# Gated Fourier mixing and attention on one core: fewer GpSimd transfers and a last head pair in two blocks

## The chip, the cores and the metric

The kernel runs on one core of a Trainium2 chip. The metric is the device time of one execution in microseconds (us), lower is better. TensorE (PE) multiplies, VectorE (DVE), ScalarE (ACT) and GpSimd (POOL) do the rest, SyncE (SP) and now and then ACT and POOL issue transfers. Each engine works off its own instructions in the order in which the program has them.

## The reference

One input x of 2048 rows and 512 columns goes through two branches that are mixed by a gate of each row:

```python
a = x @ dft_hid_re.T ; b = x @ dft_hid_im.T
y = dft_seq_re @ a - dft_seq_im @ b            # Fourier branch
q, k, v = split(x @ wqkv)                      # 32 heads of 16 columns
p = softmax(q @ k.T * 16**-0.5)                # 2048 x 2048 for each head
o = concat(p @ v) @ wo                         # attention branch
g = sigmoid((x * gate_w).sum(-1))
out = g * y + (1 - g) * o
```

All is float32. The kernel splits operands of most products into a high and a low part (`hi_lo`, L74), so one product of the reference is three on PE.

## The kernel before, in words

**Head pairs and units.** Two heads are a pair `p` (16 pairs). The stacks `qs[p % 2]` and `ks[p % 2]` hold the two heads in rows 0 to 49 and 64 to 113: 48 rows of high and low parts and two rows (48 and 49) that subtract the row's maximum. In `ks` these two rows are ones, written once (L282) before the first pair. In `qs` they are filled for each pair and each half of 1024 queries by `m_rows` (L262): DVE transposes the maxima into `mt`, then eight transfers of 2 KB (four blocks `b`, two heads `h`) go into the stack, those of head 0 from SP and those of head 1 from POOL.

A unit `u` is one pair, one half of the queries and one tile of 128 keys: 512 units (`UNITS`) in all. `scores` (L690) makes four score tiles of 128 keys by 512 queries for a unit, two heads by two query blocks, and ACT takes their exponential into `pt`. `pv` (L701) multiplies the four with the values, each into its own 32 columns of PE (four run side by side), and adds up in the PSUM bank `acc` over the 16 key tiles of a half. Row 16 of a head's values is one, so `acc` also has the sums for the softmax. Then ACT copies `acc` to `oe` and it goes to DRAM.

**PSUM.** Eight banks: three `s` (scores of head 0, and of both heads in the main part), three `a` (first maxima, at the end scores of head 1), one `acc`, one `d` (the products that fill the gaps).

**What fills the gaps.** Until unit 491 the maxima of the next pair and the Fourier branch run between the scores; `segment` places them by patterns. The results of the Fourier branch, already times the gate, are in `yg_d`. In the last part the attention's output is multiplied with `wo`, in column tiles `ct` of four pairs each: `proj(hf, cts, pools)` (L592) yields, for each of the eight row tiles of a half, three products for each `ct`, and `finish` (L583) takes the bank, scales it with 1 - g and adds it to the row tile `yp`. `first` is the half 0 with `ct` 0 to 2, `third` the half 1 with `ct` 3 without the last pair, `last` the half 0 with `ct` 3 (then the row tile is written out). `more` gives them the banks d, a, a in turn.

**The order at the end.** After the patterns four single scores remain, then the loop over u = 492, 494, ..., 510. I call one turn of it a section: half of the scores of two units, a number of products by the table `whole`, the other half, and the values of the two units before. `run_plan(u)` (L772) issues what is due: at 486 to 494 `last_block` for half 1, at 498 and 500 the sums and their reciprocals of the last column tile of half 0, at 506 its parts, at 500 `load_w15`, the four rows of `wo` that belong to the last pair.

**The last pair's second half** is not written to DRAM. `last_pair` copies `acc`, turns it so that queries are in the partitions, divides by the sums, turns it back, splits it in high and low, and multiplies with `w15`: eight row tiles, three products each, two at a time in two banks on two groups of 32 rows. Four of the eight tiles are scaled by ACT and added by POOL, the others by DVE, and SP writes all eight. Nine of `last`'s products are put between the steps, three more before the last step.

At the start `warm_up` (L131) lets DVE clear a tile, with which PE then multiplies nine times before the first inputs are there; POOL makes `ident`, the unit matrix.

Of the kernel before, what the change touches and what calls it, by code (L numbers as in the profile page):

```python
# [9 lines left out]
F32 = mybir.dt.float32  # L10
# [5 lines left out]
P = 128  # L16
# [15 lines left out]
def mix_kernel(ctx: ExitStack, tc: tile.TileContext, xa_t, xa, wqkv, w_hid, w_seq, wo, gate_w, out):  # L32
# [229 lines left out]
    def m_rows(p, hf):  # L262

        nc.vector.transpose(mt[hf], nhl[hf].rearrange("p v m -> p (v m)").bitcast(F32))  # L264
        for b in range(4):
            for h in range(2):
                rows = qs[p % 2][64 * h + 48:64 * h + 50, hf * 1024:(hf + 1) * 1024].bitcast(F32)
                (nc.sync, nc.gpsimd)[h].dma_start(rows.rearrange("v (q b c) -> v b q c", q=8, b=4)[:, b],  # L268
                                                  mt[hf][32 * b + h:32 * b + 32:2])

    def run_deferred():
        while deferred:
# [3 lines left out]
    ones = st1.tile([2, 2 * D], F32, name="hl", bufs=4)  # L276
    nc.gpsimd.memset(ones, 1.0)
    nc.gpsimd.memset(vt[:, :, :, 16:17], 1.0)
    for i in range(2):
        for h in range(2):  # L280
            for tb in range(2):
                nc.gpsimd.dma_start(ks[i][64 * h + 48:64 * h + 50, tb * 2 * D:(tb + 1) * 2 * D].bitcast(F32), ones)  # L282
    load_stacks(0)
    wos = [staged(wo[:, kt]) for kt in range(KT)]
    wrs = []
    a_next = 0

# [290 lines left out]
                parts(t[:, 0], t[:, 1], o)  # L578
                oh[hf, 3] = tiles(t)

    last_few = []

    def finish(ps, t, y, other=False):  # L583
        if other:

            tmp = last_few[0][:, t % 4]
            nc.scalar.activation(tmp, ps, AF.Copy, scale=omg[:, t:t + 1])
            nc.gpsimd.tensor_tensor(y, y, tmp, ALU.add)
            return
        nc.vector.scalar_tensor_tensor(y, ps, omg[:, t:t + 1], y, op0=ALU.mult, op1=ALU.add)  # L590

    def proj(hf, cts, pools):  # L592

        for qt in range(8):
            t = hf * 8 + qt
            chain = Chain(*pools[qt % len(pools)], 3 * len(cts))
            for ct in cts:
                h1, l1 = oh[hf, ct][qt]
                for i, (st, mv) in enumerate(((h1, 0), (h1, 1), (l1, 0))):
                    last = ct == cts[-1] and i == 2  # L600
                    yield chain, st, wos[0][:, mv, ct], partial(proj_next, hf, cts, t, chain) if last else None

    def proj_next(hf, cts, t, chain):
        finish(chain.ps, t, yp[t], last_few)
        if hf == 0 and cts[-1] == 3:
            nc.sync.dma_start(out[t * P:(t + 1) * P, :], yp[t])

# [14 lines left out]
    w15 = []  # L622

    def load_w15():
        w = work.tile([64, 2, D], F32R, name="w15")
        for i in range(4):
            nc.sync.dma_start(w[16 * i:16 * i + 16].bitcast(F32), wo_d[3][64 * (i % 2) + 3:64 * (i % 2) + 64:4])
        w15.append(w)

    def last_pair(fill):  # L630
        oe = work.tile([P, 4, P], F32, name="oe", bufs=2)
        on = work.tile([P, 4, 2, 2, DH], F32, name="on15")
        rc = work.tile([P, 4, 2, 2], F32, name="rc15")
        o15 = work.tile([64, 2, 4, P], F32R, name="o15", tag="pt", bufs=4)
        last_few.append(work.tile([P, 4, D], F32, name="few", tag="pt", bufs=4))
        w = w15[0]
        for c in range(4):
            nc.scalar.copy(oe[:, c], acc[:, c * P:(c + 1) * P])

        def turn(cs):  # L640
            t = psS.tile([P, 512], F32, name="s")
            for i, c in enumerate(cs):
                nc.tensor.transpose(t[:, i * P:(i + 1) * P], oe[:, c], ident)
            v = t[:, :2 * P].rearrange("p (c b r) -> p c b r", c=2, b=2)
            r = rc[:, cs.start:cs.stop]
            nc.vector.reciprocal(r, v[:, :, :, 16:48:16])
            for h in range(2):
                nc.vector.tensor_tensor(on[:, cs.start:cs.stop, :, h], v[:, :, :, 33 * h:33 * h + DH],
                                        r[:, :, :, h:h + 1].broadcast_to([P, 2, 2, DH]), ALU.mult)

        def back(cs):
            t = psS.tile([P, 512], F32, name="s")
            for i, c in enumerate(cs):
                nc.tensor.transpose(t[:64, i * P:(i + 1) * P], on[:, c].rearrange("p b h d -> p (b h d)"), ident)
            v = t[:64, :2 * P].rearrange("p (c q) -> p c q", c=2)
            hi_lo(o15[:, 0, cs.start:cs.stop], o15[:, 1, cs.start:cs.stop], v)

        lo, hi = range(0, 2), range(2, 4)
        pump(fill, 3)
        pump(fill, 3)  # L660
        turn(lo)
        turn(hi)
        back(lo)
        pump(fill, 3)
        back(hi)
        drain(fill)
        for c in range(4):
            pss = [(psA if b or c % 2 else psD).tile([P, 512], F32, name="a" if b or c % 2 else "d") for b in range(2)]
            for i, (st, mv) in enumerate(((0, 0), (0, 1), (1, 0))):
                for b in range(2):  # L670
                    rr = slice(32 * b, 32 * b + 32)
                    nc.tensor.matmul(pss[b], o15[rr, st, c], w[rr, mv], start=i == 0, stop=i == 2)
            for b in range(2):
                t = 8 + 4 * b + c
                y = yp.pop(t)
                finish(pss[b], t, y, b and c % 2 == 0)
                nc.sync.dma_start(out[t * P:(t + 1) * P, :], y)


    def gate():  # L680
# [9 lines left out]
    def scores(u, qb, h, other=False):  # L690
        p, r = divmod(u, 32)
        hf, kt = divmod(r, 16)
        q0 = hf * 1024 + qb * 512
        if u not in pts:
            pts[u] = work.tile([P, 4, 512], F32, name="pt", bufs=4)
        ps = psA.tile([P, 512], F32, name="a") if other else psS.tile([P, 512], F32, name="s")
        rr = slice(64 * h, 64 * h + 50)
        nc.tensor.matmul(ps, ks[p % 2][rr, kt * P:(kt + 1) * P], qs[p % 2][rr, q0:q0 + 512], start=True, stop=True)  # L698
        return nc.scalar.activation(pts[u][:, 2 * qb + h], ps, AF.Exp, bias=0.0, scale=DH ** -0.5)  # L699

    def pv(u, evac=True):  # L701
        p, r = divmod(u, 32)
        hf, kt = divmod(r, 16)
        pt = pts.pop(u)
        for j in range(4):
            h = j % 2
            nc.tensor.matmul(acc[32 * j:32 * j + 17], vt[:, kt, p, 16 * h:16 * h + 17], pt[:, j],  # L707
                             start=kt == 0, stop=kt == NT - 1)
        if kt == NT - 1 and evac:
# [216 lines left out]
```

## Time and profile before

| | us |
|---|---|
| three runs, median (lowest to highest) | 1725.36 (1724.99 to 1726.66) |
| the profiled execution | 1726.38 |
| its span, first to last instruction | 1724.3 |

| engine | busy us in the profiled execution | instructions |
|---|---|---|
| PE | 1713.2 | 13018 |
| DVE | 1364.3 | 2296 |
| ACT | 1149.4 | 2256 |
| POOL | 446.5 | 562 |

Times in the views are counted from the start of the span. A row of a timeline has the start, the length, the engine, the line, the operation and its tiles (out<-in), a count, and in brackets how long the engine stood idle before it and what ended that. "SPq" and "POOLq" rows, and POOL's DMA_DIRECT2D rows, are issues of transfers. The chain of waits is the path that ended last: start, length, engine, tile, line. PE's rows in a timeline overlap, as matmuls are pipelined; in the chain each has only what it adds.

### The profile page before, as it was taken

The numbers are of one execution on the slowest core, as the hardware profiler recorded it, in microseconds if no ns is written. First come the engines' busy times: TensorE is split into PE (matmuls) and PEld (weight loads), VectorE is DVE, ScalarE is ACT, GpSimd is POOL, SyncE is SP. The second block draws the span as 40 slices with busy tenths as digits, with TensorE's granted clock in tenths as the row PEclk, the third lists the DMA queues.
The fourth block names the chain that finished last, engine by engine and source line by source line (L and its number), as shares of the span: only waits on it lengthen the run. The fifth ranks groups of instructions, "written<-read, shape, count | busy, mean of one in ns | idle before, by whom it ended". The sixth has DMA issues, their size and how long they took to land.

```text
span 1724.3 us, 33482 instructions
## 1 busy us (share of the span) xinstructions
PE 1713.2 (99%) x13018; PEld 1043.1 (60%) x13018; DVE 1364.3 (79%) x2296; ACT 1149.4 (67%) x2256; POOL 446.5 (26%) x562
## 2 busy tenths in 40 slices
PE   9999999999999999999999999999999999999998
PEld 7888655456666666666666666666666666544443
DVE  5439788888888888888888888888888888799953
ACT  5211377777766777677767777777677777777776
POOL 0111121322222333222322333333232343200111
PEclk9999999999999999999999999999999999999999
DMA  8963500314141524214146535233141534460103
GB/s 290 347 145 141 136 7 14 44 38 75 56 75 45 96 87 101 72 35 78 39 92 246 114 100 104 62 66 66 45 89 61 125 100 93 169 153 24 39 27 129
DMA packets 82350, 164.82 MB, mean 96 GB/s; under 512 B 19712, under 2 KB 19968, under 8 KB 78352
## 3 DMA queue, kind: packets, MB, share of 16 engines
q1 hardware_dynamic: 77552, 161.77, 36.6%
q8 instruction: 102, 1.67, 0.4%
q0 software_dynamic: 4352, 0.39, 0.3%
q10 hardware_dynamic: 288, 0.52, 0.1%
q14 instruction: 56, 0.46, 0.1%
HBM read 107.47 MB, written 54.52 MB: 94 GB/s over the span
## 4 chain that ended last, share of the span: by engine, by line
PE 98%; DVE 0%; DMA 0%; ACT 0%; issue 0%; POOL 0%; DVEq 0%; ACTq 0%; POOLq 0%
PE d L410 35%; PE acc L707 28%; PE a L245 12%; PE s L698 12%; PE s L324 3%; PE s L356 1%; PE d L324 1%; PE a L81 1%; PE a L79 1%; PE s L81 1%; PE s L79 1%; PE a L80 1%; PE s L80 1%; PE a L410 0%; PE s L203 0%; PE a L203 0%
## 5 line engine op out<-in xcount | busy, mean ns | idle before, releaser
L247 DVE TENSOR_REDUCE mx<-a 128x1 f32<-128x512 f32 x2026 | 1246.4, 683 | 244.4 <-PE a L245 222.2
L699 ACT ACTIVATE pt<-s 128x512 f32<-128x512 f32 x2008 | 1024.1, 620 | 389.5 <-PE s L698 332.4
L245 PE MATMUL a<-ks,qs 48*128 48x512 f32 x2026 | 813.3, 416 | 0.0
L698 PE MATMUL s<-qs,ks 50*128 50x512 f32 x2008 | 770.0, 413 | 1.6 <-DMA qs<-mt 1.2
L410 PE MATMUL d<-xab,ch 64*128 64x512 f32 x2016 | 648.5, 396 | 0.0
L707 PE MATMUL acc<-pt,vt 128*17 128x512 f32 x4096 | 500.7, 596 | 0.0
L410 PEld LDWEIGHTS d<-xab,ch 64*128 64x128 f32 x2016 | 365.9, 184 | 126.9 <-DVE mx L247 60.4
L698 PEld LDWEIGHTS s<-qs,ks 50*128 50x128 f32 x2008 | 366.1, 184 | 111.0 <-ACT pt L699 33.7
L245 PEld LDWEIGHTS a<-ks,qs 48*128 48x128 f32 x2026 | 367.7, 185 | 66.8 <-DVE mx L247 40.2
L410 PE MATMUL d<-xab,cl 64*128 64x512 f32 x1008 | 399.3, 396 | 0.0
L410 PEld LDWEIGHTS d<-xab,cl 64*128 64x128 f32 x1008 | 185.4, 184 | 65.5 <-DVE mx L247 40.8
L394 POOL CAST ch<-craw 128x512 fp32r<-128x512 f32 x126 | 77.2, 612 | 558.3 <-PE s L698 192.0
L707 PEld LDWEIGHTS acc<-pt,vt 128*17 128x17 f32 x4096 | 90.6, 96 | 205.9 <-issue 205.9
L395 POOL TENSOR_TENSOR cl<-craw,ch 128x512 fp32r<-128x512 f32 x126 | 162.4, 1289 | 10.2
L268 POOL DMA_DIRECT2D qs<-mt x128 | 72.0, 568 | 158.2 <-DVE mt L264 150.0
L410 PE MATMUL d<-wre,xab 64*128 64x512 f32 (+1 forms) x348 | 93.9, 402 | 0.1
L410 PEld LDWEIGHTS d<-wre,xab 64*128 64x128 f32 (+1 forms) x348 | 60.0, 185 | 32.0 <-issue 23.6
L410 PE MATMUL d<-wo_hl,o_hl 64*128 64x512 f32 (+1 forms) x261 | 70.9, 397 | 0.0
L410 PEld LDWEIGHTS d<-wo_hl,o_hl 64*128 64x128 f32 (+1 forms) x261 | 47.2, 185 | 16.9 <-issue 11.7
L75 ACT CAST hl<-s 128x512 fp32r<-128x512 f32 x28 | 16.2, 588 | 59.7 <-PE d L324 25.2
L259 POOL CAST nhl<-nm 128x16 fp32r<-128x16 f32 x32 | 6.3, 197 | 160.8 <-DVE nm L256 160.8
L427 POOL CAST xab<-y 128x512 fp32r<-128x512 f32 x16 | 9.8, 610 | 129.8 <-ACT y L426 107.2
(147 smaller groups left out, 967.8 us busy)
## 6 DMA issues: line engine op xcount, KB each, us to landing
craw<-w_seq SPq DMA_DIRECT2D x128, 256.0 KB
qk<-hl SPq DMA_DIRECT2D x32, 512.0 KB
qs<-qk SPq DMA_DIRECT2D x96, 128.0 KB
ks<-qk SPq DMA_DIRECT2D x96, 128.0 KB
b<-hl SPq DMA_DIRECT2D x16, 512.0 KB
xab<-b SPq DMA_DIRECT2D x16, 512.0 KB
o<-oe SPq DMA_DIRECT2D x62, 128.0 KB
oh<-nh SPq DMA_DIRECT2D x12, 512.0 KB
```

The source lines that it names most:

```text
L79: nc.tensor.matmul(ps, sh, mh, start=first, stop=False)
L80: nc.tensor.matmul(ps, sh, ml, start=False, stop=False)
L245: nc.tensor.matmul(ps, qs[p % 2][r, qt * P:(qt + 1) * P], ks[p % 2][r, kb * 512:(kb + 1) * 512], start=True, stop=True)
L247: user = nc.vector.tensor_reduce(mx[p % 2][:, h, qt, kb:kb + 1], ps, AX.X, ALU.max)
L268: (nc.sync, nc.gpsimd)[h].dma_start(rows.rearrange("v (q b c) -> v b q c", q=8, b=4)[:, b], mt[hf][32 * b + h:32 * b + 32:2])
L324: i = nc.tensor.matmul(ps, st[r], mv[r], start=not half and not j, stop=half == 1 and j == 11)
L394: nc.gpsimd.tensor_copy(h1, raw)
L395: nc.gpsimd.tensor_tensor(l1, raw, h1.bitcast(F32), ALU.subtract)
L410: i = nc.tensor.matmul(self.ps, st[r], mv[r], start=not self.begun, stop=stop)
L698: nc.tensor.matmul(ps, ks[p % 2][rr, kt * P:(kt + 1) * P], qs[p % 2][rr, q0:q0 + 512], start=True, stop=True)
L699: return nc.scalar.activation(pts[u][:, 2 * qb + h], ps, AF.Exp, bias=0.0, scale=DH ** -0.5)
L707: nc.tensor.matmul(acc[32 * j:32 * j + 17], vt[:, kt, p, 16 * h:16 * h + 17], pt[:, j], start=kt == 0, stop=kt == NT - 1)
```

## The change

**Transfers.** The eight transfers of ones go from POOL to SP, behind the first pair's stacks. In `m_rows` POOL issues those of head 1 only if the group is neither the first nor the last of all, and for the first pair only three of four. So POOL issues 30 groups of four less one, 119 transfers in all, and SP issues the 17 others.

**The last sections.** `proj` gets a list of row tiles. `first` and `last` leave out row tile 7, which is done apart: three products (`early`) at 504 and nine (`late`) behind the last values. Five of `first`'s products go between the third and the fourth of the single scores. The table `whole` has other numbers.

**The last pair by blocks of 512 queries.** Units 496 to 511 run through all 16 key tiles for the first 512 queries and then for the second: a unit there is two key tiles by one query block, and `acc` holds, for each head, the even and the odd key tiles apart. A constant `pairsum`, two unit matrices of 64 one above the other, made by DVE, adds the two while the block is turned (`turn`). Block 0 (`LastPair(0)`) is copied after unit 503, turned in section 506, turned back in 508 and multiplied before the last two units' values; block 1 follows behind them. Its products use four groups of 32 rows, one for each row tile and each with its own bank, and `w15` stands four times in 128 partitions (eight transfers instead of four). One tile of block 1 goes by ACT and POOL and is written by ACT's queue, and the kept row tile 7 is added by DVE in between.

```diff
+    pairsum = const.tile([P, 64], F32, name="pairsum")
+    nc.vector.tensor_tensor(pairsum, ident[:, :64], ident[:, 64:], ALU.add)
...
+                own = h and 0 < 2 * p + hf < 2 * NP - 1 and (p or b < 3)
                 rows = qs[p % 2][64 * h + 48:64 * h + 50, hf * 1024:(hf + 1) * 1024].bitcast(F32)
-                (nc.sync, nc.gpsimd)[h].dma_start(rows.rearrange("v (q b c) -> v b q c", q=8, b=4)[:, b],
-                                                  mt[hf][32 * b + h:32 * b + 32:2])
+                (nc.gpsimd if own else nc.sync).dma_start(rows.rearrange("v (q b c) -> v b q c", q=8, b=4)[:, b],
+                                                            mt[hf][32 * b + h:32 * b + 32:2])
...
+    load_stacks(0)
+    wos = [staged(wo[:, kt]) for kt in range(KT)]
     for i in range(2):
         for h in range(2):
             for tb in range(2):
-                nc.gpsimd.dma_start(ks[i][64 * h + 48:64 * h + 50, tb * 2 * D:(tb + 1) * 2 * D].bitcast(F32), ones)
-    load_stacks(0)
-    wos = [staged(wo[:, kt]) for kt in range(KT)]
+                nc.sync.dma_start(ks[i][64 * h + 48:64 * h + 50, tb * 2 * D:(tb + 1) * 2 * D].bitcast(F32), ones)
...
+    class LastPair:
...
+        def copy(self, n):
+            for c in range(n):
+                cols = slice(c * 512 // n, (c + 1) * 512 // n)
+                nc.scalar.copy(self.oe[:, cols], acc[:, cols])
+
+        def turn(self):
+            t = self.bank(0)
+            for c in range(4):
+                nc.tensor.matmul(t[:, 64 * c:64 * c + 64], self.oe[:, c * P:(c + 1) * P], pairsum, start=True, stop=True)
+            v = t[:, :256].rearrange("p (c r) -> p c r", c=4)
+            nc.vector.reciprocal(self.rc, v[:, :, 16:48:16])
+            for h in range(2):
+                nc.vector.tensor_tensor(self.on[:, :, h], v[:, :, 33 * h:33 * h + DH],
+                                        self.rc[:, :, h:h + 1].broadcast_to([P, 4, DH]), ALU.mult)
+
+        def back(self):
+            t = self.bank(1)
+            nc.tensor.transpose(t[:, :P], self.on.rearrange("p c h d -> p (c h d)"), ident)
+            hi_lo(self.o15[:, 0], self.o15[:, 1], t[:, :P])
+
+        def products(self, pools, order, others=()):
+            pss = [pool.tile([P, 512], F32, name=name) for pool, name in pools]
+            for i, (st, mv) in enumerate(((0, 0), (0, 1), (1, 0))):
+                for c in range(4):
+                    r = slice(32 * c, 32 * c + 32)
+                    nc.tensor.matmul(pss[c], self.o15[r, st], w15[0][r, mv], start=i == 0, stop=i == 2)
+            for c in order:
+                t = 8 + 4 * self.blk + c
+                y = yp.pop(t)
+                finish(pss[c], t, y, c in others)
+                (nc.scalar if c in others else nc.sync).dma_start(out[t * P:(t + 1) * P, :], y)
...
     def last_pair(fill):
...
+        few.append(work.tile([P, D], F32, name="few", tag="pt", bufs=4))
+        x = LastPair(1, [(psS, "s")])
+        x.copy(4)
+        pump(fill, 1)
+        x.turn()
+        pump(fill, 5)
+        x.back()
         drain(fill)
+        x.products([(psA, "a")] * 3 + [(psD, "d")], (1, 2, 0, 3), (0,))
...
+        if u >= UNITS - 16:
+            blk, kt = divmod(kt, 8)
+            q0, kt = 1024 + blk * 512, 2 * kt + qb
...
+    def pv_last(u):
+        blk, k2 = divmod(u - UNITS + 16, 8)
+        pt = pts.pop(u)
+        for j in range(4):
+            x, h = divmod(j, 2)
+            nc.tensor.matmul(acc[32 * j:32 * j + 17], vt[:, 2 * k2 + x, NP - 1, 16 * h:16 * h + 17], pt[:, j],
+                             start=k2 == 0, stop=k2 == 7)
+        if blk == 0 and k2 == 7:
+            last_pairs.append(LastPair(0, [(psD, "d"), (psA, "a")]))
+            last_pairs[0].copy(1)
...
-    first = proj(0, (0, 1, 2), one)
+    first = proj(0, (0, 1, 2), one, range(7))
...
     for i in range(4):
+        if i == 3:
+            pump(first, 5)
         score("s", 1)
...
-    last = proj(0, (3,), more)
-    whole = {492: (first, 9), 494: (first, 9), 496: (first, 9), 498: (third, 6), 500: (third, 6), 502: (third, 6),
-             504: (third, 3), 506: (third, 3), 508: (last, 6), 510: (last, 6)}
+    last = proj(0, (3,), more, range(7))
+
+    early, late = proj(0, (0,), one, (7,)), proj(0, (1, 2, 3), [(psS, "s")], (7,))
+    whole = {492: (first, 4), 494: (first, 9), 496: (third, 9), 498: (third, 3), 500: (third, 9), 502: (third, 3),
+             504: (early, 3), 508: (last, 9), 510: (last, 12)}
...
-                pump(*whole[u])
+                pump(*whole.get(u, ((), 0)))
+                if u == 506:
+                    last_pairs[0].turn()
+                elif u == 508:
+                    last_pairs[0].back()
...
+    last_pairs[0].products([(psA, "a")] * 3 + [(psD, "d")], range(4))
     pv(UNITS - 2)
-    pv(UNITS - 1, evac=False)
-    last_pair(last)
+    pv(UNITS - 1)
+    last_pair(late)
```

More of the change, by code (lines that the diff above doesn't have):

```diff
@@ L579, in last_block @@
                 oh[hf, 3] = tiles(t)
-    last_few = []
+    few = []
     def finish(ps, t, y, other=False):
         if other:
-            tmp = last_few[0][:, t % 4]
+            tmp = few[0]
             nc.scalar.activation(tmp, ps, AF.Copy, scale=omg[:, t:t + 1])
@@ L590, in finish, with proj @@
         nc.vector.scalar_tensor_tensor(y, ps, omg[:, t:t + 1], y, op0=ALU.mult, op1=ALU.add)
-    def proj(hf, cts, pools):
-        for qt in range(8):
+    def proj(hf, cts, pools, qts=range(8)):
+        for qt in qts:
             t = hf * 8 + qt
@@ L603, in proj_next @@
     def proj_next(hf, cts, t, chain):
-        finish(chain.ps, t, yp[t], last_few)
+        finish(chain.ps, t, yp[t])
         if hf == 0 and cts[-1] == 3:
@@ L624, in load_w15 @@
     def load_w15():
-        w = work.tile([64, 2, D], F32R, name="w15")
-        for i in range(4):
+        w = work.tile([P, 2, D], F32R, name="w15")
+        for i in range(8):
             nc.sync.dma_start(w[16 * i:16 * i + 16].bitcast(F32), wo_d[3][64 * (i % 2) + 3:64 * (i % 2) + 64:4])
         w15.append(w)
-    def last_pair(fill):
[L631 to L665, printed above, removed]
-        drain(fill)
[L667 to L677, printed above, removed]
@@ new lines, in mix_kernel, with __init__, bank @@
+    class LastPair:
+        def __init__(self, blk, pools):
+            self.blk, self.pools = blk, pools
+            self.oe = work.tile([P, 512], F32, name="oe", bufs=2)
+            self.on = work.tile([P, 4, 2, DH], F32, name="on15", bufs=2)
+            self.rc = work.tile([P, 4, 2], F32, name="rc15", bufs=2)
+            self.o15 = work.tile([P, 2, P], F32R, name="o15", bufs=2)
+        def bank(self, i):
+            pool, name = self.pools[i % len(self.pools)]
+            return pool.tile([P, 512], F32, name=name)
+        def copy(self, n):
[26 more added lines that the diff above has]
+                (nc.scalar if c in others else nc.sync).dma_start(out[t * P:(t + 1) * P, :], y)
@@ L699, in scores, with pv @@
         return nc.scalar.activation(pts[u][:, 2 * qb + h], ps, AF.Exp, bias=0.0, scale=DH ** -0.5)
-    def pv(u, evac=True):
+    def pv_last(u):
[8 more added lines that the diff above has]
+            last_pairs[0].copy(1)
+    def pv(u):
+        if u >= UNITS - 16:
+            return pv_last(u)
         p, r = divmod(u, 32)
@@ L708, in pv @@
                              start=kt == 0, stop=kt == NT - 1)
-        if kt == NT - 1 and evac:
+        if kt == NT - 1:
             oe = work.tile([P, 512], F32, name="oe", bufs=2)
```

1 line of the change is left out of this document (added).

## The prediction

> **What bounds the kernel now.** I read the page first, then the waits of TensorE (PE), then the chain of waits and the timelines at both ends.
>
> ```profile
> span 1724.3 us, 33482 instructions
> PE 1713.2 (99%) x13018; PEld 1043.1 (60%) x13018; DVE 1364.3 (79%) x2296; ACT 1149.4 (67%) x2256; POOL 446.5 (26%) x562
> 1654.75:1708.84 54.09, 53.42 (x325) 22.87 (x324) 16.82 (x25) 43.55 (x85) 4.97 (x7) 1.00 0.19 51
> 1708.84:1724.30 15.46, 7.95 (x44) 5.19 (x44) 6.04 (x14) 5.46 (x12) 7.51 (x6) 0.77 0.53 204
> ```
>
> The last two rows are stretches of the span: length, then busy time of PE, weight loads, DVE, ACT and POOL, then clock and DMA. PE is busy 99% of the span, so PE work that goes, or a stop of PE that goes, comes off the time. PE stops in three places: at the start, once in the middle, and in the 15.46 us behind the last product with the values (T0 = 1708.84), of which it works half. The change touches all three, and the ten sections before T0. The profiled execution took 1726.38 us, 1.02 above the median of 1725.36; I sum against it and carry the difference over to the median.
>
> **GpSimd's transfers.** From the timelines of POOL, PE and SP:
>
> ```profile
> 99.83 4.29 POOL L282 DMA_DIRECT2D ks<-hl  x8 [5.50 <-DMA qk<-hl]
> 175.11 1.22 POOL L268 DMA_DIRECT2D qs<-mt  x2 [2.27 <-DVE mt L264]
> 1428.09 2.26 POOL L268 DMA_DIRECT2D qs<-mt  x4 [5.67 <-DVE mt L264]
> 1475.72 1.71 POOL L268 DMA_DIRECT2D qs<-mt  x3 [2.70 <-DVE mt L264]
> 1480.07 0.56 POOL L268 DMA_DIRECT2D qs<-mt  x1 [2.64 <-issue]
> 1485.34 0.47 PE L698 MATMUL s<-qs,ks 50*128 50x512 f32 x1 [1.23 <-DMA qs<-mt]
> 1655.55 2.38 POOL L568 TENSOR_TENSOR o_raw<-o_raw 128x1024 f32<-128x1024 f32 x1
> 1655.71 2.75 SPq L268 DMA_DIRECT2D qs<-mt  x4
> L268 POOL DMA_DIRECT2D qs<-mt x128: 561/561/634, 175.1 to 1659.6; - x128
> ```
>
> Eight transfers of ones go out, then four for each half of a head pair: 27 such groups from 175 to 1428 and three of the next, so 8 + 108 + 3 = 119 stand before the issue that pauses 2.64 us for nothing the profile shows. The 120th's data is what PE then waits 1.23 us for. The four groups behind it are regular. If the count of issues brings the pause, 119 in all never reach it: **-1.2 us**, between -1.23 and 0; it can't cost, for the issues left are the same ones.
>
> The 17 others join SP's queue at 2.75 / 4 = 0.69 us each. The ones and the first rows are read only once scores begin. Of the last group, POOL's four began behind L568, at 1657.9, and were out at 1660.2; eight on SP are out at 1655.7 + 8 x 0.69 = 1661.2. Their first reader, unit 496, begins near 1667 (sum below), so issue and landing have some 6 us of cover; what SP does next, unit 495's accumulator, comes later still. Nothing; beyond that cover each us would be one of PE's.
>
> **The start.** `pairsum` precedes, on DVE, the memset that feeds the warm-up, and it needs `ident`:
>
> ```profile
> 0.92 0.48 DVE L134 MEMSET xab<- 128x512 f32 x1 [0.92 <-PEq L919]
> 1.02 0.29 POOL masks.py:199 TENSOR_SCALAR_AFFINE_SELECT ident<-ident 128x128 f32<-128x128 f32 x1
> 1.46 4.21 PE d L137 x9
> 6.80 0.43 PE s L203
> 7.49 0.23 PE s L203
> ```
>
> `ident` is there at 1.31. The addition of 128x64 isn't in this trace; two 128x64 products take 0.37 (below), so 0.2 for one. The memset moves from 0.92 to about 1.55, and the nine warm-ups end at 6.3 instead of 5.67, ahead of the first real product. PE is dense behind that: **+0.6**. Were the full clock (0.23 a product, not 0.43) to come at the same moment as now, only half would be lost: 0.3 to 0.7.
>
> **The last sections.** A section is two units: scores, products with `wo`, scores, values.
>
> ```profile
> 1655.22 0.61 ACT pt L699
> 1657.35 2.26 PE d L410 x9
> 1659.62 0.42 PE s L698
> 1660.04 0.23 PE s L698
> 1660.28 1.84 PE acc L707 x16
> 1673.65 0.90 PE d L410 x3
> 1490.03 4.03 ACT L699 ACTIVATE pt<-s 128x512 f32<-128x512 f32 x8
> 1679.81 0.55 DVE L517 RECIPROCAL rc<-rc 128x64 f32<-128x64 f32 x1 [3.77 <-DMA rc<-o]
> 1680.92 0.21 PE a L698
> 1692.72 2.06 ACT pt L699 x4
> 1705.28 3.56 PE acc L707 x32
> ```
>
> Each half of scores is 0.42 + 0.23 = 0.65, values 1.84, n products 0.2 + 0.23n (0.90 for 3, 2.26 for 9). So a section with 9 takes 5.4, one with 3 takes 4.05, one with 12 takes 6.1. ACT needs 3.9 for its eight exponentials (0.48 apart) and is hidden unless a bank is missing: the `a` banks go round in threes, so one product tile in `a` makes the section's fourth `a` score wait for the second `a` exponential, about 2.55 into the section. That is the 2.06 row: a section with three products took 4.9.
>
> After, in order:
> - Four single scores and 492: five products go between the third and fourth score, where PE now waits 0.61 for ACT and then runs at ACT's pace. Scores 0.91, products 1.35, scores 0.9, four products 1.1, scores 0.65, values 1.84: 6.8.
> - 494 and 496, nine each: 10.8. 498, three in `d`: 4.05.
> - 500, nine: its fourth `a` score waits for a product tile that DVE adds behind the reciprocal. As now (the 0.21 row follows it), but that reciprocal comes 0.5 earlier, with its data: 5.95.
> - 502, three in `a`: 4.9. 504, three in `d`: 4.05.
> - 506, no products: four fold matmuls (by the row below, 0.5) and 0.1 of waiting for block 0's copy: 4.1.
> - 508, nine, one transpose (0.25) and a bank of DVE's to wait for (0.2): 5.85. 510, twelve: 6.1.
> - Block 0's last products, 12 on four row groups: 0.42 + 0.23 + 0.23 = 0.9 if four groups overlap as two do now. Then values, 1.84.
>
> Sum 55.3 against 54.09: T0 comes **1.2 us later**, though three more products, the fold and block 0's ending lie ahead of it. Bounds: -0.6 if 500, 502 and 508 don't wait; +3.7 if 498 and 504 take 4.9 too and the four groups go two by two (0.7).
>
> The Trainium skill ("TensorE: Matmul & The Clock Gate", Part 3, Measured speedup vs the span model) gives 3.07 times for four row groups, not 4. An estimate by it: 12 x 0.23 / 3.07 + 0.2 = 1.1, so 0.2 more at each of the two places. The trace has pairs only.
>
> **The tail**, in us behind T0:
>
> ```profile
> 1708.98 0.77 ACT L638 COPY oe<-acc 128x128 f32<-128x128 f32 x4 [2.00 <-PE acc L707]
> 1710.42 0.23 PE s L643 x2
> 1710.67 0.22 DVE rc L646
> 1710.92 0.37 DVE on L648 x2
> 1711.83 0.37 ACT L75 CAST o<-s 64x256 fp32r<-64x256 f32 x1 [0.68 <-PE s L654]
> 1712.23 0.42 DVE L76 TENSOR_TENSOR o<-s,o 64x256 fp32r<-64x256 f32 x1 [0.45 <-ACT o L75]
> 1714.30 2.10 DVE yp L590 x3
> 1714.49 1.27 POOL L588 TENSOR_TENSOR yp_ks<-yp_ks,few 128x512 f32<-128x512 f32 x1
> L677 SPq DMA_DIRECT2D out<-yp x8: 332/402/507, 1716.2 to 1720.0; - x8
> ```
>
> Now eight tiles wait for one pair's products, each in its own bank and row pair, and the last issue starts at 1720.0: 11.16 behind T0, 4.3 before the span's end. After, only four and the tile kept back remain. Copies end at 0.9; the fold of the last chunk at 1.2; reciprocal and scaling (0.6) at 1.85, while five products run to 2.4; transpose to 2.65; the high half by ACT 2.95, the low half by DVE 3.3, while the last three products run to 3.35; twelve products to 4.25. DVE adds the kept tile from 3.4 to 4.1 and three more, 0.70 each, to 6.4; the fifth, ACT 0.7 and POOL 1.27, is done at 6.25 and goes out by ACT's queue, idle by then. Last issue 6.45, end 6.45 + 4.3 = 10.75 instead of 15.46: **-4.7**. Bounds: -5.3 (the 4.3 held transfers queued behind each other) to -3.9 (row groups two by two).
>
> **Sum.** -1.2 + 0.6 + 1.2 - 4.7 = -4.1. Profiled 1722.3; median 1725.36 - 4.1 = **1721.3**.
>
> **The rivals.**
> - The pause comes anyway, by time or by state and not by count. Against: one in 136 issues. 1721.3 + 1.2 = 1722.5. The Trainium skill's "DMA: Bandwidth & Descriptors" (Issuing engines are not separate DMA queues) points here: another issuer saves only sequencer time. The 2.64 us speak against it. Chance 0.09.
> - Banks: 498, 504 and 510 wait as 502 does, 0.85 each: 1723.9. For: the 2.06 row. Against: two of them use no `a` product tile. 0.11.
> - The full clock comes a whole stretch later because PE starts later. From 1.46 to 7.23 is 5.8 us; once more at 0.43 for 0.23 loses 2.7: 1724.0. The Trainium skill ("TensorE: Matmul & The Clock Gate", Part 1) has a free-running window, which allows this or no loss at all; the one run here can't tell. 0.05.
> - Row groups run singly: 12 x 0.23 + 0.2 = 2.96 for 0.9, twice: 1725.4, no gain. Against: pairs overlap fully. 0.04.
> - The other side: with nine products after one half, exponentials no longer run beneath the values, for all banks are taken. Each of the nine sections 494 to 510 becomes 0.65 + 3.9 + 1.84 = 6.4 instead of 5.1 on average: +11.8, 1733.1. It turns slower than before once they average over 5.5. For: the 2.06 row. Against: ACT idles 10.5 us of the 54.09. 0.07.
>
> **How the numbers follow.** The forecast has 0.64, its own range 1719.9 to 1722.6. A measurement of this kernel can tell about 0.2%, 3.5 us, from no change, so faster means under 1721.9: some six sevenths of the forecast, 0.56. Within 0.2%: the rest of it and the first four rivals, 0.37. Slower: the last, 0.07. The range, 1719.4 to 1724.2, leaves out the last two rivals and some 0.08 of the edges.
>
> **What would show it.** No POOL issue with a pause, and no PE wait for qs<-mt; the first warm-up near 2.1; T0 near 1709.5 (1710.0 by the sections, less the pause, plus the start); sections of 5.4 and 4.05 in turn; twelve products at the end within 0.9; the last issue 6.4 behind T0. A T0 beyond 1712, or a tail over 13, would prove it wrong.

## The result, and the profile after

| | before | after |
|---|---|---|
| median us (lowest to highest) | 1725.49 (1724.17 to 1727.79) | 1721.61 (1720.91 to 1722.41) |
| runs | 17 | 17 |
| the profiled execution; its span | 1726.38; 1724.3 | 1721.80; 1720.0 |

After is 0.9975 of before, 95% interval 0.9968 to 0.9982: 3.9 us faster. The forecast was 1721.3, range 1719.4 to 1724.2.

The head of the page of after, and the same two stretches as in the prediction, cut at after's own moments (last single scores to T0, T0 to the end):

```profile
span 1720.0 us, 33483 instructions
PE 1711.0 (99%) x13028; PEld 1045.6 (61%) x13028; DVE 1367.3 (79%) x2302; ACT 1146.0 (67%) x2252; POOL 431.9 (25%) x540
1653.31:1709.86 56.55, 55.67 (x348) 24.99 (x348) 21.48 (x36) 43.91 (x87) 2.81 (x3) 1.00 0.25 70
1709.86:1720.00 10.14, 4.42 (x30) 2.99 (x30) 4.40 (x10) 1.73 (x6) 1.27 (x1) 0.87 0.57 219
```

The sections are 2.46 longer than before's 54.09, the tail is 5.32 shorter than 15.46, and the sections begin 1.44 earlier. That is the whole 4.3 by which the span is shorter.

GpSimd's timeline in after, at the groups that answer to 1428 and 1475 of before and at one later group, and then all of PE's waits in after:

```profile
1428.22 2.27 POOL L273 DMA_DIRECT2D qs<-mt  x4 [5.67 <-DVE mt L267]
1475.83 2.27 POOL L273 DMA_DIRECT2D qs<-mt  x4 [2.69 <-DVE mt L267]
1568.73 1.14 POOL L273 DMA_DIRECT2D qs<-mt  x2 [4.97 <-DVE mt L267]
1572.40 1.13 POOL L273 DMA_DIRECT2D qs<-mt  x2 [2.53 <-issue]
```

```profile
PE d L140 <- DVE xab L137: 2.2, 1, 2.2
PE a L720 <- ACT pt L721: 0.4, 1, 0.4
PE d L658 <- ACT oe L652: 0.3, 1, 0.3
```

The group at 1475.83 now goes out in one piece and PE waits for no row. But the pause has not gone: it stands two groups later, ahead of GpSimd's 114th issue, where nobody waits for it: between the transpositions before and behind it the kernel after takes 45.40 us (1568.23 to 1613.63), and the kernel before, without a pause there, 45.41 (1569.67 to 1615.08).

That the pause was dear in before has a second reason, which the prediction did not see. The row issued at 1480.07 came behind four loads of 512 KB that SP had issued, and is the one that took longest of GpSimd's 128 from issue to landing (the second line has the smallest, the median and the largest time in us):

```profile
1478.88 2.57 SPq L494 DMA_DIRECT2D wo_hl<-wo  x4
DMA to landing us min/median/max: 1.7/1.7/5.1
```

1480.07 + 5.1 = 1485.2, and PE's wait ends at 1485.34. With 1.7 the row would have been there at 1481.8, before PE came for it at 1485.34 - 1.23 = 1484.1. While the row was under way, 259 to 321 GB/s were moving (1480 to 1486). In the kernel after, the two rows behind the pause land in 1.7 us, where next to nothing else moves (1 to 5 GB/s).

After's tail, from its timeline:

```profile
1709.92 0.77 ACT L652 COPY oe<-acc 128x128 f32<-128x128 f32 x4 [2.99 <-PE acc L728]
1711.39 0.21 DVE L660 RECIPROCAL rc<-s 128x8 f32<-128x8 f32 x1 [0.80 <-PE s L658]
1713.41 0.75 DVE L595 SCALAR_TENSOR_TENSOR yp_ks<-s,omg,yp_ks 128x512 f32<-128x512 f32 x1
1714.33 1.41 DVE L595 SCALAR_TENSOR_TENSOR yp<-a,omg,yp 128x512 f32<-128x512 f32 x2 [0.17 <-PE d L677]
1715.66 0.74 DVE L595 SCALAR_TENSOR_TENSOR yp<-d,omg,yp 128x512 f32<-128x512 f32 x1
1715.12 1.27 POOL L593 TENSOR_TENSOR yp<-yp,few 128x512 f32<-128x512 f32 x1 [58.62 <-DVE yp L595]
1716.42 0.38 ACTq L682 DMA_DIRECT2D out<-yp  x1
```

DVE adds the kept tile and three more, one goes by ACT and POOL, and the last issue starts 6.56 behind T0 (1709.86).

**A yardstick for single profiles.** Executions with the same instructions up to there differ by up to 1.0 us before the first pair begins (174.17 to 175.19 in seven profiles), because PE's clock opens at another moment: the two earliest of them to open are also the two earliest at the first pair. The chain of waits at the start, of after and of the kernel with 113 transfers (further down), which have the same instructions there:

```profile
2.17 4.21 PE d L140 x9
7.23 0.30 PE s L206
7.54 0.24 PE a L206
```

```profile
7.66 0.43 PE a L206
8.08 0.24 PE s L206
```

A product takes 0.43 until the clock is full and 0.23 from then on; in the 14 profiles of this study the first full one begins between 5.9 and 7.9 where the warm-up began at 1.46 (mean 6.6), and between 6.2 and 8.1 where it began at 2.17 (mean 7.4). The Trainium skill ("TensorE: Matmul & The Clock Gate", Part 1) has a free-running window behind this, with some 0.5 us of variation to each side; the spread here, 2.0 and 1.9 us from first to last, is about twice that. So I compare single profiles by the part of the span behind the first transposition of maxima, which lies behind all that. It is this row, of before and of after:

```profile
174.61 0.20 DVE L264 STREAM_TRANSPOSE mt<-nhl 128x32 f32<-128x32 f32 x1
```

```profile
174.85 0.20 DVE L267 STREAM_TRANSPOSE mt<-nhl 128x32 f32<-128x32 f32 x1
```

Behind it before takes 1724.3 - 174.61 = 1549.7 and after 1720.0 - 174.85 = 1545.2: 4.5 less. In the experiments this is called the rest of the span. It is read from one profile of each kernel.

### The profile page after: what moved, and what is told of

It reads as the page before. It is cut to its first block, busy times and chain, and to the rows that moved or that the text cites. A ratio compares the mean times of both kernels' runs of the same rounds, so it can differ in the third digit from the quotient of the medians.

```text
span 1720.0 us, 33483 instructions
## 1 busy us (share of the span) xinstructions
PE 1711.0 (99%) x13028; PEld 1045.6 (61%) x13028; DVE 1367.3 (79%) x2302; ACT 1146.0 (67%) x2252; POOL 431.9 (25%) x540
## 3 DMA queue, kind: packets, MB, share of 16 engines
q0 software_dynamic: 3808, 0.30, 0.2%
## 4 chain that ended last, share of the span: by engine, by line
PE 99%; ACT 0%; DVE 0%; issue 0%; DVEq 0%; POOL 0%; POOLq 0%; ACTq 0%
PE d L415 36%; PE acc L742 27%; PE a L248 12%; PE s L720 12%; PE s L329 3%; PE s L361 1%; PE d L329 1%; PE acc L728 1%; PE a L84 1%; PE a L82 1%; PE s L84 1%; PE s L82 1%; PE a L83 1%; PE s L83 1%; ACT pt L721 0%; PE s L206 0%
## 5 line engine op out<-in xcount | busy, mean ns | idle before, releaser
L742 PE MATMUL acc<-pt,vt 128*17 128x512 f32 x3968 | 485.6, 596 | 0.0
L273 POOL DMA_DIRECT2D qs<-mt x119 | 67.2, 570 | 155.3 <-DVE mt L267 147.5
```

The lines of the kernel that those rows point to most:

```text
L273: (nc.gpsimd if own else nc.sync).dma_start(rows.rearrange("v (q b c) -> v b q c", q=8, b=4)[:, b], mt[hf][32 * b + h:32 * b + 32:2])
```

## Experiments on GpSimd's transfers

**The new split alone.** Before, with the new `own` in `m_rows` and the ones on SP behind the stacks.

```diff
-                (nc.sync, nc.gpsimd)[h].dma_start(
+                own = h and 0 < 2 * p + hf < 2 * NP - 1 and (p or b < 3)
+                (nc.gpsimd if own else nc.sync).dma_start(
...
-                nc.gpsimd.dma_start(ks[i][...].bitcast(F32), ones)
+                nc.sync.dma_start(ks[i][...].bitcast(F32), ones)
```

> The kernel before with the new split of the small transfers alone (119 issues by GpSimd). Theory I (GpSimd stops once, near its 891st instruction, whatever that is): the pause is there, 2.5 us long, before the third or fourth issue of the group that begins near 1570 us, as in the kernel after; TensorE has no wait for qs<-mt; 1725.4 - 1.5 = 1723.9 us. Theory R (a ring of descriptors fills, the eight transfers of ones together counting about two rows): the same place and time, 1723.9. Theory C of the prediction (the 120th issue): no pause anywhere, 1724.2.

Measured 1725.31 (11 runs), 0.9997 of before (0.9988 to 1.0006), where the theories wanted 1723.9 or 1724.2. Its timeline of GpSimd:

```profile
1568.07 1.13 POOL L269 DMA_DIRECT2D qs<-mt  x2 [4.96 <-DVE mt L264]
1571.73 1.12 POOL L269 DMA_DIRECT2D qs<-mt  x2 [2.53 <-issue]
```

The pause moves ahead of the 114th issue by this part alone, and PE's wait for the rows is gone. The rest of the span is 1722.8 - 174.06 = 1548.7, 0.95 less than before; the medians of the spans differ by 0.65 (1722.9 and 1723.55) and those of the times by 0.18, which the interval can't tell from nothing. At the place itself the trace shows more: between the transpositions around the pause of before, the kernel before takes 49.01 us (1475.22 to 1524.23) and this kernel 47.48 (1474.66 to 1522.14), 1.5 less; 0.6 of that goes again in the last sections and the tail. The split is worth at most a us in all, then, and the times alone don't show that it is worth anything.

**More instructions on GpSimd.** 14 one-column memsets near 100 us in before, 20 in after, to see if the pause counts instructions.

```diff
+    for i in range(14):
+        nc.gpsimd.memset(pad[:, i:i + 1], 0.0)
```

> The kernel before with all its 136 transfers on GpSimd and 14 one-column memsets more on GpSimd near 100 us, where it is idle. Theory I: the 891st instruction is now a split of a Fourier chunk near 1465 us, where GpSimd idles 9 us anyway; no pause among the transfers, no wait of TensorE for qs<-mt, 1723.9 us. Theories R and C: the pause stays before the 120th issue and TensorE waits 1.2 us, 1725.4 us.

> The kernel after with 20 one-column memsets more on GpSimd near 100 us: the 104th to 107th issue are then its 889th to 892nd instruction, as the 117th to 120th were before. Theory I: the pause comes back inside the group near 1476 us, at the 106th or 107th issue, and TensorE waits about 1.2 us for qs<-mt; 1721.6 + 1.5 = 1723.1 us. Theory R: the pause stays at the 114th issue near 1570 us, 1721.6. Theory C: no pause, 1721.6.

Measured 1726.51 (0.0 to 0.17% slower than before) and 1721.52, 11 runs each. The two timelines:

```profile
1478.85 0.56 POOL L269 DMA_DIRECT2D qs<-mt  x1 [2.64 <-issue]
```

```profile
1572.63 1.13 POOL L274 DMA_DIRECT2D qs<-mt  x2 [2.54 <-issue]
```

The pause is still ahead of the 120th issue in the one and of the 114th in the other. It is not instructions, and not the count of issues either. With 8 transfers of ones the pause comes behind 111 row transfers, without them behind 113: eight ones count as two rows.

**Fewer on GpSimd: 111, 113, 115.** The limit in `own` moved down, so that SP issues eight, six or four more.

```diff
-                own = h and 0 < 2 * p + hf < 2 * NP - 1 and (p or b < 3)
+                own = h and 0 < 2 * p + hf < 2 * NP - 3 and (p or b < 3)             # 111
+                own = h and 0 < 2 * p + hf < 2 * NP - 3 + (b < 2) and (p or b < 3)   # 113
+                own = h and 0 < 2 * p + hf < 2 * NP - 2 and (p or b < 3)             # 115
```

> The changed kernel with two more groups of row transfers on SP: GpSimd issues 111 instead of 119. Theory R (GpSimd stops once, before the 114th row transfer where the ones go by SP and before the 112th where they went by GpSimd, and in the changed kernel nothing waits for it): no issue with an idle time of 2.5 us before it, and the time stays within 0.3 of the changed kernel's 1721.61. Rival (the stop costs in the changed kernel too, unseen, by what DVE or SP then do later): 0.5 to 1.5 faster, 1720.1 to 1721.1. Rival (eight more issues on SP, 0.69 us each, now delay its other transfers): 0.5 or more slower.

> The changed kernel with GpSimd issuing 113 row transfers instead of 119. With 111 the time was 6.2 longer, all of it behind the last DMA byte: 7.7 us from there to the span's end instead of 1.4, with no engine at work. Theory E (GpSimd has to stop once, when its ring of descriptors has gone round; a program that ends before the 114th row transfer has not stopped and pays at the end instead): 113 don't reach the stop, no idle time of 2.5 us before an issue, 5.5 to 6.5 us longer than the changed kernel, 1727.1 to 1728.1. Rival Q (the end is longer because SP's queue has more transfers, each of the eight moved costing 0.8): six moved, 4.6 longer, 1726.2. Rival L (the end is longer because GpSimd's last transfer lies 91 us further from the end): half of 111's price or less, 1721.6 to 1724.7.

> The changed kernel with GpSimd issuing 115 row transfers, two beyond the stop. Theory E: the stop comes before the 114th, near 1572, the end takes 1.4 us behind the last byte as in the changed kernel, and the time is within 0.7 of 1721.61. Rival Q (SP's queue, 0.8 for each transfer moved): four moved, 1724.7. Rival L (distance of GpSimd's last transfer from the end): between 1721.6 and 1727.8, nearer to the kernel with 113 than to that with 119, as its last transfer lies in the same group.

| GpSimd's row transfers | us | rest of the span | pause |
|---|---|---|---|
| 111 | 1727.83 (11 runs) | 1726.5 - 175.04 = 1551.5 | none |
| 113 | 1728.26 (8) | 1727.0 - 175.19 = 1551.8 | none |
| 115 | 1722.07 (8) | 1719.7 - 174.17 = 1545.5 | before the 114th |
| 119 (after) | 1721.61 (17) | 1545.2 | before the 114th |

For 111 no theory foresaw 6.2 slower; only the last rival, SP's queue, has the sign. The second and third kernels were made to tell what the price hangs on; theory E foretold both, though 1728.26 lies 0.2 above its range. GpSimd's timeline with 113 (its last issues) and with 115:

```profile
1569.25 1.13 POOL L273 DMA_DIRECT2D qs<-mt  x2 [4.96 <-DVE mt L267]
```

```profile
1568.17 1.13 POOL L273 DMA_DIRECT2D qs<-mt  x2 [4.96 <-DVE mt L267]
1571.83 1.12 POOL L273 DMA_DIRECT2D qs<-mt  x2 [2.53 <-issue]
```

The end of after and of the kernel with 111, in stretches of 1 us (PE, weight loads, DVE, ACT, POOL, then clock, DMA's share and GB/s):

```profile
1718.00:1719.00 1.00, 0.00 (x0) 0.00 (x0) 0.00 (x0) 0.00 (x0) 0.00 (x0) 0.50 0.64 242
1719.00:1720.00 1.00, 0.00 (x0) 0.00 (x0) 0.00 (x0) 0.00 (x0) 0.00 (x0) 0.50 0.00 0
```

```profile
1718.50:1719.50 1.00, 0.00 (x0) 0.00 (x0) 0.00 (x0) 0.00 (x0) 0.00 (x0) 0.50 0.32 119
1719.50:1720.50 1.00, 0.00 (x0) 0.00 (x0) 0.00 (x0) 0.00 (x0) 0.00 (x0) 0.50 0.00 0
...
1725.50:1726.50 1.00, 0.00 (x0) 0.00 (x0) 0.00 (x0) 0.00 (x0) 0.00 (x0) 0.50 0.00 0
```

With 111 the last byte is written at about 1718.8, as in after but for 0.2, and then nothing runs for 7.7 us, where after has 1.4. One row of SP's waits near the end differs, at L966, where the block of the whole kernel ends. It is first that of after, then that with 111 (us in all, times, longest):

```profile
SPq L966 <- PEq L966: 0.7, 2, 0.5
```

```profile
SPq L966 <- PEq L966: 6.9, 2, 6.5
```

With 113 it is 7.0 us. So the long end is one wait at the program's close; that PE's sequencer is named need not be the cause, as PE had long been done. Two row transfers more, the 114th and 115th, take 6.2 us off. A price for each transfer on SP (4.6, then 3.1 by that theory) and one for the distance of GpSimd's last issue are both out, as 113 and 115 end in the same group. Of the kernels here that let GpSimd issue rows, each had the pause, 2.5 to 2.6 us, or paid more than twice as much at its end.

**None on GpSimd.** The version without bank waits (below) with every row transfer on SP.

```diff
-                (nc.gpsimd if own else nc.sync).dma_start(
+                nc.sync.dma_start(
```

> The version without bank waits (1720.15) with all row transfers on SP: GpSimd issues none. With 111 and 113 on GpSimd there was no stop and the end behind the last byte took 7.7 instead of 1.4 us; with 115 and 119 there was the stop and a short end. Theory E1 (the end is long whenever the stop has not come before it, also where GpSimd issued nothing): 6.0 to 6.5 longer, 1726.2 to 1726.7. Theory E2 (the long end belongs to transfers of GpSimd that no stop has followed; with none there is nothing to pay): 1720.0 to 1720.4, and a margin on top if SP's 0.69 for each of eight transfers in place of four, 2.7 us later, makes PE wait for the rows: PE waited 1.2 for them in the kernel before at 2.1 us of delay, so up to 30 groups by up to 1.5 us if they have that little cover everywhere, and nothing if the two groups that went by SP in the kernel with 111, which showed no wait, are typical.

Measured 1721.55 (11 runs), 0.9980 of before (0.9971 to 0.9989); there is no pause, and the span ends 1.4 us behind the last byte, as in after. So the long end belongs to GpSimd transfers that no pause has followed. The rest of the span, 1719.2 - 173.62 = 1545.6, is 1.1 above that of the version it was made from, and the time 1.4. By the later transpositions all of it arises between 238 and 380 us, 0.4 to 0.5 in each of three halves of a pair, and nothing is added behind. PE's waits show no row there, so its cause stays open.

What is counted stays open too. The Trainium skill ("DMA: Bandwidth & Descriptors", SWDGE vs HWDGE vs iDMA) says that GpSimd writes its descriptors into rings in SBUF; a ring that has gone round would fit, but no run shows one, and the packets of its queue don't fit: 4352 for 136 transfers and 3808 for 119, 32 for each, ones and rows alike, though eight ones count as only two rows.

## Experiments on the start, the sections and the tail

**`pairsum` behind the warm-up's memset.**

```diff
-    nc.vector.tensor_tensor(pairsum, ident[:, :64], ident[:, 64:], ALU.add)
...
         warm_up()
+        nc.vector.tensor_tensor(pairsum, ident[:, :64], ident[:, 64:], ALU.add)
```

> The kernel after with the sum of the two unit matrices made behind the memset of the warm-up. If the full clock comes at a moment of its own (about 7.5 us in both traces), the start gives back 0.1 to 0.3 us: 1721.4. If it counts from TensorE's first work: 0.6 us, 1721.0.

Measured 1721.28 (10 runs), 0.3 below after, with intervals that overlap. The profiles say more. The first transposition lies at 173.6 to 174.8 in the seven with the memset first (mean 174.12) and at 174.2 to 175.2 in the seven with `pairsum` first (mean 174.82): 0.7 for the start. Each seven spread over 1.0 to 1.2 us, so the price of the start lies between 0.3 and 0.7 and isn't settled.

**The two blocks alone.** Before with `LastPair`, `pv_last` and the four row groups; transfers, table and tile order as before; the end is filled with twelve of `last`'s products. Against after, the last line of the edit is:

```diff
-    last_pair(late)
+    last_pair(last)
```

> The kernel before with the last pair by two blocks of 512 queries alone (pairsum, pv_last, four row groups): transfers, table of products and tile order as before, no tile kept back, no products between the single scores; twelve of last's products fill the end instead of nine. By the prediction's terms: start +0.6, fold, transpose and block 0's products +1.95 ahead of T0, tail -4.0 (the -4.7 less three products and a second DVE addition, 0.7): -1.45, so 1724.0. By the trace of the changed kernel: start +0.1, fold 1.1, transpose and wait 0.45, products 1.17, tail -4.6: -1.8, so 1723.7. The pause before GpSimd's 120th issue stays. Rival (the blocks do it all: the new table and the kept tile give nothing): 1721.6 to 1722.6, as the changed kernel plus the pause. Rival (the end isn't where the time went): 1725.3 or more.

Measured 1724.71 (11 runs), 0.9995 of before (0.9986 to 1.0004): 0.7 and 1.0 above the two sums and in neither rival's range. The rest of the span is 1723.6 - 175.13 = 1548.5, 1.2 less than before. The chain of waits in its tail (T0 = 1710.84):

```profile
1712.97 1.37 DVE yp_qs L595 x2
1714.33 0.20 DVE o L79
1714.53 0.66 DVE yp_qs L595
1715.19 0.67 DVE yp_ks L595
1716.72 0.75 DVE yp L595
```

The twelve products are four row tiles, so DVE adds four tiles there instead of one, and the block's own low half (`o`) queues among them. The tail takes 12.76, 2.6 more than after's.

**The kept tile and the table alone.** Before with `early`, `late`, the new table and the five products between the single scores.

```diff
+        if i == 3:
+            pump(first, 5)
...
+    early, late = proj(0, (0,), one, (7,)), proj(0, (1, 2, 3), [(psS, "s")], (7,))
+    whole = {492: (first, 4), 494: (first, 9), 496: (third, 9), 498: (third, 3), 500: (third, 9), 502: (third, 3),
+             504: (early, 3), 508: (last, 9), 510: (last, 12)}
...
+    last_pair(late)
```

> The kernel before with the new table, the five products between the single scores and the tile kept back, and nothing else: the last pair's second half in one piece as before, transfers as before. The two blocks alone gave 1724.71, 0.8 below before; what is left of the 3.9 is 3.1. Theory K (the kept tile is worth most of it, in the tail, since nine products are then added by one DVE addition instead of three, 0.7 us each, and two 256 KB writes less wait behind them; the blocks only make room): about 2 to 3 below before, 1722.5 to 1723.5, by a tail 1.5 to 2.5 shorter. Rival S (the two only help together: in one piece the eight tiles of the last pair still go one behind the other and DVE's saved additions only let it wait): within 0.8 of before, 1724.7 to 1726.3.

Measured 1724.10 (11 runs), 0.9994 of before (0.9985 to 1.0003); the rest of the span is 1721.8 - 173.74 = 1548.1, 1.6 less than before. It lies between the two theories. Its tail is 14.31 (T0 = 1707.49): eight tiles are still written at the end, and near its end only the writes run, at some 400 GB/s:

```profile
1716.80:1717.80 1.00, 0.00 (x0) 0.00 (x0) 0.19 (x1) 0.00 (x0) 0.00 (x0) 0.50 1.06 410
1717.80:1718.80 1.00, 0.00 (x0) 0.00 (x0) 0.00 (x0) 0.00 (x0) 0.00 (x0) 0.50 1.05 404
1718.80:1719.80 1.00, 0.00 (x0) 0.00 (x0) 0.00 (x0) 0.00 (x0) 0.00 (x0) 0.50 1.04 399
```

By the rest of the span the parts add up to 0.95 + 1.2 + 1.6 = 3.8 of the 4.5; by the median times to 0.2 + 0.8 + 1.2 = 2.2 of the 3.9, and no part alone can be told from nothing by its interval. So the parts together give more than the sum, by 0.7 to 1.7 us. The tails show why. The blocks take the writes of half the tiles out of the end, the kept tile takes three DVE additions out, and each alone leaves the other limit (tails of 12.76 and 14.31, against 15.46 before and 10.14 with both).

**Six products instead of nine and three in turn.**

```diff
-    whole = {492: (first, 4), 494: (first, 9), 496: (third, 9), 498: (third, 3), 500: (third, 9), 502: (third, 3),
+    whole = {492: (first, 4), 494: (first, 9), 496: (third, 6), 498: (third, 6), 500: (third, 6), 502: (third, 6),
```

> The changed kernel with six products in each of 496 to 502 instead of nine and three in turn. Theory A (nine and three in turn save bank waits: a section with products in one a bank waits for ACT whatever their number): a section of six takes 4.97 and up to 5.3, four of them 19.9 to 21.2, against 20.4 measured for 496 to 502 of the changed kernel; with the reciprocal's wait of 500 on top the time is 0.2 to 0.9 longer, 1721.8 to 1722.5. Rival (the turn is worth nothing, the products fill the same time in any order): within 0.2 of 1721.61. Rival (even sections are better, as six products of 1.58 lie wholly beneath ACT's 3.9): 0.3 to 0.8 shorter, 1720.8 to 1721.3.

Measured 1721.74 (11 runs), 0.13 above after: the turn is worth nothing that can be told. Its sections 496 to 502 take 20.3 us, those of after 20.4.

**Without bank waits.** `pairsum` late, `third` and `last` into other banks, the reciprocal of 500 and the rows of `wo` later.

```diff
-    third = proj(1, (3,), more)
-    last = proj(0, (3,), more, range(7))
+    third = proj(1, (3,), more + more + one + one)
+    last = proj(0, (3,), more[1:] + one, range(7))
...
-        at(last + (12 if ct < 3 else 4), inverse, hf, ct, n)
+        at(last + (12 if ct < 3 else 4 if hf else 6), inverse, hf, ct, n)
...
-    for step, u in enumerate((500, 506, 506)):
+    for step, u in enumerate((502, 506, 506)):
...
-    at(500, load_w15)
+    at(504, load_w15)
```

> The changed kernel with the waits of its sections for banks and for DVE taken away: pairsum made behind the warm-up; the product tiles of third and last put into other banks (502 uses d instead of a, 508 leaves its fourth a score a free bank); the reciprocal that holds up 500 issued one section later, with its data's step and the last rows of wo. Theory B (the sections took 56.55 us, not the 55.3 of the prediction, because 500, 502 and 508 wait for a bank or for DVE, 0.45, 0.9 and 0.3 over the 5.4, 4.05 and 5.8 that their products take, and the fold of 506 is bound by ACT): the sections get 1.2 to 1.7 shorter, with the start 0.1 to 0.3 earlier the time is 1.4 to 1.9 below the changed kernel's 1721.61: 1719.7 to 1720.2. Rival P (the sections are as long as PE's own work and the waits only move from one section to the next, ACT's eight exponentials of 3.9 us plus 1.84 of values being the floor): only the start's 0.1 to 0.3 comes: 1721.3 to 1721.5.

Measured 1720.15 (7 runs), 0.9971 of before (0.9960 to 0.9982): 1.5 below after's median, but the two intervals overlap. The rest of the span is 1719.3 - 174.82 = 1544.5, 0.7 less than after's. The sections take 55.64 (1653.49 to 1709.13), 0.9 less, where the theory wanted 1.2 to 1.7. By the starts of the values 502 takes 4.06 (after 4.98), 500 5.77 (5.90), 508 5.89 (6.12), and 510 6.53 (6.11): a product tile of 510 now waits for ACT, in the chain of waits:

```profile
1700.12 1.09 ACT pt L721 x2
```

So most of the waits went and one came back in 510. Six of the seven runs lie below the lowest of after's seventeen (1720.91), so the better version is likely, but the intervals don't show it.

## Why the prediction was right, step by step

**GpSimd's transfers, -1.2.** The size came out near, 0.95 by the rest of the span, by luck: the reason was wrong. The wait of PE went; the sections begin 1.44 earlier. But the step "if the count of issues brings the pause, 119 in all never reach it" fell: the pause came, ahead of the 114th. The gain came because it fell on rows that land in 1.7 us, while those of before came behind SP's loads and took 5.1. "It can't cost, for the issues left are the same ones" fell as well: six fewer would have cost 6.6. The rival "the pause comes anyway" was right on the pause and wrong on the price. The rule behind it, that another issuer saves only the sequencer's time ("DMA: Bandwidth & Descriptors", Issuing engines are not separate DMA queues, in the Trainium skill), does not hold for this case, where two transfers between issuers move the end by 6.2.

**The start, +0.6.** Not settled: the profiles have 0.7 in the mean, the direct experiment 0.3, and the prediction's own alternative was 0.3 to 0.7. The two executions shown differ by only 0.24, since before's clock opened late in its own. The rival with a whole stretch of slow clock more did not come: in no profile is the clock full later than 8.1.

**The sections, +1.2, measured +2.46.** This lies within its bounds (-0.6 to +3.7), and was mis-sized by 1.2, of which three terms make 1.1. In the chain of waits of after:

```profile
1688.39 2.10 ACT pt L721 x4
1690.48 0.49 ACT oe L652
1691.02 1.10 PE d L658 x8
1696.22 2.14 DVE yp L595 x3
1698.40 0.50 PE a L720
1706.85 0.63 PE a L677 x3
1708.02 1.84 PE acc L728 x16
```

The fold was to take 0.5 and takes 1.10, as its four float32 products show as eight matmuls (x8), and it waits for ACT's copy: 504 and 506 took 8.69, not 8.15. In 508 the fourth `a` score waits for DVE's additions: 6.12, not 5.85. The twelve products of block 0 took 1708.02 - 1706.85 = 1.17, not 0.9; there the estimate by the Trainium skill's 3.07 times ("TensorE: Matmul & The Clock Gate", Part 3, Measured speedup vs the span model), 1.1, was the nearer. The rest came within 0.1 of the list: 492 6.78, 494 and 496 10.9, 498 4.07, 500 5.89, 502 4.98, 510 6.11. So neither the rival on banks nor the one on row groups came, and the other side, exponentials that no longer hide, is far off: the nine sections 494 to 510 average 5.2.

**The tail, -4.7, measured -5.3.** The last issue starts 6.56 behind T0, by the sum 6.45; the way from there to the end is 3.6 where 4.3 was held over from before, as only one tile is still queued behind another. That the kept tile saves DVE time is in the sum; the kernel with the blocks alone shows that without it the tail would be 2.6 longer.

**Sum.** -1.2 + 0.6 + 1.2 - 4.7 = -4.1 against -3.9 of the medians. In the profiles -1.44 (transfers and start), +2.46 and -5.32 give -4.3: the sections' error is made good by the tail's and by the late clock of before's profile, so that the sum came within 0.2 is in part luck.

## What to carry to other kernels

Price the end of a kernel by its last writer, its last adder and its last product one by one: here two parts that were worth 1.2 and 1.6 alone, by one profile each, are worth 0.7 or more beyond that together, since each alone leaves another limit. Compare single profiles from a point behind the start, where the clock has opened. And where GpSimd issues transfers, look for a pause and for idle time behind the last byte: move a few transfers between issuers and time it, in both directions.

## What the runs showed of the hardware

GpSimd's issues pause once, 2.53 to 2.64 us, behind 113 row transfers of 2 KB or behind 111 and eight of ones, in all eleven kernels that issue so many; a program with 111 or 113, which has not paused, ended 6.2 to 6.7 us later, with no engine and no DMA at work, and one with none paid neither. A row of 2 KB from GpSimd lands in 1.7 us in the median and took 5.1 behind four loads of 512 KB. PE's clock was full from a moment between 5.9 and 8.1 us, and the first pair came at 173.6 to 175.2.

The 17 runs of before spread over 3.6 us and those of after over 1.5. Part of that lies outside the span, where no trace reaches: the time less the span is 1.7 to 3.3 us in 32 runs of before, and at most 1.92 in every run of the ten kernels with the blocks. By the means (2.10 and 1.82) some 0.3 us of the gain lies there too. Why is open.
